# All queries formed ahead of the first iteration, and the last stores on one queue: an attention block with its gradients on one core

## The chip, the core and the metric

The kernel runs on one NeuronCore of a Trainium2 chip. The core has five engines, each with its own instruction queue, that meet only at semaphores: TensorE (PE; its weight loads are shown apart, as PEld), VectorE (DVE), ScalarE (ACT), GpSimd (POOL) and SyncE (SP). Data moves between HBM and the on-chip memory (SBUF) by 16 DMA engines, which serve several queues; here SP's DMAs run in queue q1, ScalarE's in q10 and GpSimd's, whose descriptors are made by software, in q0. TensorE writes to PSUM, eight banks for each partition.

The metric is the time of one execution in microseconds of device time, the median of several runs. Lower is better.

## What is computed

One decode step (one new token for each of two sequences) of a pre-norm transformer block, and its gradients for everything that was put in. Cut to what matters:

```python
B, Sq, D = 2, 1, 640; H, Sk, Dh = 32, 4096, 128; Dff = 1728      # all in bf16
q = layernorm(x) @ wq                       # wq: 640 x 4096, 32 heads of 128
s = q . k_cache * Dh**-0.5                  # for each sequence and head, over 4096 keys
p = softmax(s);  o = p . v_cache
h = x + o @ wo
out = h + relu(layernorm(h) @ w1) @ w2
# and the vector-Jacobian product with grad_out for x, k_cache, v_cache, wq, wo, w1, w2
```

The caches k and v are 2 x 32 x 4096 x 128 each, 1 MB for each pair of sequence and head, and so are their gradients (outputs 2 and 3). These four arrays are nearly all of the bytes moved. Output 0 is the block's result and output 1 the gradient of x, both 2 x 640; outputs 4 to 7 are the gradients of the four weights.

## The kernel before

The program is written out by hand: a planner in Python walks over two interleaved loops and emits each engine's instructions in the order that it fixes. There are 64 pairs (sequence, head).

The first loop (`p1_iter(i)`, 66 iterations) is the forward pass. For pair i it turns the K tile (128 x 4096, 1 MB) over by 32 transposes on TensorE in four groups of eight (`transpose_group`, L418, copied out by ScalarE at L423 or VectorE at L421), multiplies each by the query (`matvec_group`, L429, which reads a column of `qc`) and takes the maximum (L575). One iteration later the scores of that pair become exponentials (L528) and K is scaled by them (`pk_half`, L480). Two iterations later V is multiplied with that (`m_part`, L473). So iteration i needs K of pair i, K of pair i - 1 and V of pair i - 2.

The second loop (`p2_iter(j)`) writes the gradients of the caches. It begins at iteration 41 of the first loop, at every second iteration, and runs alone after the first has ended. For pair j it reads V again (tile W, unless it was kept), turns it over (`pair_transpose`, L439, copied by ScalarE at L444), multiplies it (L452), and forms the tiles gV (of pair j) and gK (of pair j - 1) on VectorE in halves (`outer_half`, L834). GpSimd makes the small tile `pp` (L872) that gV is formed from; VectorE makes `gsp` (L856) for gK. `store_tile` (L839 to 846) sends each tile to HBM.

Between these, other generators run in the gaps: `middle_gen` (the MLP and the second layer norm of a sequence), `ga_gen`, `fin_gen` (outer products for outputs 4 to 7, stored by ScalarE from tiles `ot`), and `gx_gen`, which reads wq a second time in five tiles `wqs` (L989) and multiplies them on VectorE (L660, tile gxj) for output 1. `store_row` (L649 to 655) turns a column over and stores it as a row of output 0 or 1.

The large tiles are places in a pool of twelve, more later, divided by use: "ld" for loads, "g" for gK and gV, "f" and "q" for the others. `take` gets the place given back longest ago, and `give` returns it. A load into a place waits until the tile before it has been read, and VectorE, when it forms gK or gV, until the store of the tile that was there has landed.

All large loads are in one list, `queue`, in the order in which they are wanted, and `pump` issues from its head on SP as long as a place for loads is free: for each iteration K of pair i and V of pair i - 2, with W tiles, w2 in three pieces (iterations 8, 13, 18), wo in four and w1 (iterations 10, 15, 20, 24, 35).

wq is read in six pieces, each with the columns of six heads (`QP = 6`, the last with two): `load_wq` takes one place for loads and moves five chunks of 768 columns for each partition, runs of 1536 B. The first stands at the head of `queue`, and each other one three iterations ahead of its use. `q_piece(k)`, at iterations 0, 6, 12, 18, 24 and 30, forms the queries of its heads in 30 matmuls (L384; 10 for the last), copies them to `qc` and, scaled, to `qsc` (L388, L389), and gives the place back.

Where a store is sent from depends on the list: as long as anything is left in `queue`, gK and gV are stored by GpSimd, and once all loads are issued, by SP. Two of the last gK tiles are then stored in two parts, 120 rows and 8 rows. The rows of outputs 0 and 1 are stored by GpSimd. Engines work through their queues in order, so a store behind which another instruction stands holds that up until the tile is ready.

Of the kernel before, what the change touches and what calls it, by code (L numbers as in the profile page):

```python
# [7 lines left out]
FP32 = mybir.dt.float32  # L8
BF16 = mybir.dt.bfloat16
ALU = mybir.AluOpType  # L10
# [5 lines left out]
def kernel(  # L16
# [20 lines left out]
    nc = tc.nc  # L37

    B, Sq, D = A_x.shape
    _, H, Sk, Dh = A_k_cache.shape  # L40
    HD = A_wq.shape[1]
    Dff = B_w1.shape[1]
    assert (B, Sq, Dh) == (2, 1, 128) and H * Dh == HD
    ND = D // 128
# [4 lines left out]
    SCALE = 0.08837890625  # L49
# [17 lines left out]
    small = ctx.enter_context(tc.tile_pool(name="small", bufs=3))  # L67
# [5 lines left out]
    def pst(shape, dtype, role, name):  # L73

        k = banks[role].pop(0)
        banks[role].append(k)
        return ps.tile(shape, dtype, tag=f"bank{k}", bufs=1, name=name)
# [11 lines left out]
    def take(tag, shape, name):  # L89
        assert free[tag] > 0, (tag, name)  # L90
        free[tag] -= 1
        k = homes[tag].pop(0)
        t = pools[k].tile(shape, BF16, tag=f"big{k}", bufs=1, name=name)
        home_of[id(t)] = (tag, k, t)
        return t
# [9 lines left out]
    def give(t, to=None):  # L105
        tag, k, _ = home_of.pop(id(t))
        to = to or goes_to(tag)
        owned[tag] -= 1
        owned[to] += 1
        free[to] += 1  # L110
        homes[to].append(k)
        given_at[k] = step[0]
# [35 lines left out]
    ident_bf = const.tile([128, 128], BF16)  # L148
# [32 lines left out]
    x1c = cols.tile([128, ND, B], BF16)  # L181
# [11 lines left out]
    qsc = cols.tile([128, H, B], BF16)  # L193
# [133 lines left out]
    qc = pkp.tile([128, H, B], BF16)  # L327
# [36 lines left out]
            nc.sync.dma_start(out=t[0:F_rem, NFF - c0, :], in_=B_w2[NFF * 128:Dff, :])  # L364
        return t

    QP = 6
    NQ = -(-H // QP)
    wq_r = A_wq.rearrange("(c p) n -> p c n", p=128)
    wq_tiles = {}  # L370

    def load_wq(k, tag):
        hn = min(QP, H - k * QP)
        t = take(tag, [128, ND, QP * 128], "wq_t")
        nc.sync.dma_start(out=t[:, :, 0:hn * 128], in_=wq_r[:, :, k * QP * 128:(k * QP + hn) * 128])
        wq_tiles[k] = (t, tag)

    def q_piece(k):
        hn = min(QP, H - k * QP)
        t, tag = wq_tiles.pop(k)  # L380
        q_ps = pst([128, QP, B], FP32, "mid", "q_ps")
        for j in range(hn):
            for c in range(ND):
                nc.tensor.matmul(q_ps[:, j, :], lhsT=t[:, c, j * 128:(j + 1) * 128], rhs=x1c[:, c, :],  # L384
                                 start=(c == 0), stop=(c == ND - 1))
        give(t)
        hs = slice(k * QP, k * QP + hn)
        nc.vector.tensor_copy(out=qc[:, hs, :], in_=q_ps[:, 0:hn, :])  # L388
        nc.vector.tensor_scalar(out=qsc[:, hs, :], in0=qc[:, hs, :], scalar1=SCALE, scalar2=None, op0=ALU.mult)  # L389


    pairs = [(b, h) for b in range(B) for h in range(H)]
    NP1 = len(pairs)
# [61 lines left out]
    def natural(cache, b, h):  # L455
        return cache[b, h].rearrange("(p sc) d -> p sc d", sc=NSC)
# [192 lines left out]
    def store_row(col_bf, n, dst):  # L649

        t = pst([16, 128], BF16, "mid", "row_ps")
        nc.tensor.transpose(t[0:n, :], col_bf, ident_bf[:])
        r = small.tile([16, 128], BF16, tag="orow", bufs=2, name="orow")
        nc.vector.tensor_copy(out=r[0:n, :], in_=t[0:n, :])
        nc.gpsimd.dma_start(out=dst, in_=r[0:n, :])

    def ttr(in0, in1, acc, width, kc=128, junk=None):
        if junk is None:
# [177 lines left out]
            in0=row.rearrange("p (a two) -> p a two", two=2)[:, None, :, :].to_broadcast([128, HALF, 64, 2]),  # L836
            in1=colp[:, sl, None, :].to_broadcast([128, HALF, 64, 2]), op=ALU.mult)

    def store_tile(dst, t, uneven=False):  # L839

        eng = nc.gpsimd if queue else nc.sync
        if uneven:
            eng.dma_start(out=dst[0:120], in_=t[0:120])
            eng.dma_start(out=dst[120:128], in_=t[120:128])
        else:
            eng.dma_start(out=dst, in_=t[:])  # L846

    def p2_iter(j, busy):

        c = S2[j] if j < NP1 else None  # L850
        p = S2[j - 1] if j >= 1 else None
        if p is not None:
            bp, hp = turns[j - 1]
            pair_matvec(p["dp"], p.pop("T3"), 3, gom[:, hp, bp, :, :])
            gsp = small.tile([128, NSC, 2], BF16, tag="gsp", name="gsp")
            nc.vector.scalar_tensor_tensor(  # L856
                out=gsp[:], in0=p["dp"][:, :, None].to_broadcast([128, NSC, 2]), scalar=negdot[:, hp, bp:bp + 1],
                in1=P_bf[:, bp * H + hp, :, None].to_broadcast([128, NSC, 2]), op0=ALU.add, op1=ALU.mult)
        if c is not None:
            b, h = turns[j]  # L860
            go = gom[:, h, b, :, :]

            bank = pst([128, 512], FP32, "sps", "dp_ps")
            for k, col in enumerate((goc, qsc)):
                nc.tensor.matmul(bank[:, 128 + k * 128:256 + k * 128],  # L865
                                 lhsT=col[:, h, b:b + 1].to_broadcast([128, 128]), rhs=ident_bf[:],
                                 start=True, stop=True)
            c["dp"] = bank[:, 0:NSC]
            rb = mats.tile([128, 256], BF16, tag="rb", bufs=4, name="rb")
            nc.scalar.activation(out=rb[:], in_=bank[:, 128:384], func=ACT.Copy, scale=rt[:, b, h:h + 1])  # L870
            pp = small.tile([128, NSC, 2], BF16, tag="pp", name="pp")
            nc.gpsimd.tensor_copy(out=pp[:], in_=P_bf[:, b * H + h, :, None].to_broadcast([128, NSC, 2]))  # L872
            c.update(rb=rb, pp=pp)
            c["T0"] = pair_transpose(c["W"], 0, busy=busy)
        if p is not None:
            gK = take("g", [128, NSC, 128], "gK")
            outer_half(gK, p["rb"][:, 128:256], gsp, 0)
        yield
        if p is not None:
            outer_half(gK, p["rb"][:, 128:256], gsp, 1)  # L880
            store_tile(natural(out_2, bp, hp), gK, NP1 - 3 <= j - 1 < NP1 - 1)
            give(gK)
            del S2[j - 1]
        yield
        if c is None:
            return
        c["T1"] = pair_transpose(c["W"], 1, busy=busy)
        pair_matvec(c["dp"], c.pop("T0"), 0, go)
        yield
        c["T2"] = pair_transpose(c["W"], 2, busy=busy)  # L890
        pair_matvec(c["dp"], c.pop("T1"), 1, go)
        yield
        c["T3"] = pair_transpose(c["W"], 3, busy=busy)
        give(c["W"], "g" if j < H and j != 1 and owned["g"] < 3 else None)
        pair_matvec(c["dp"], c.pop("T2"), 2, go)
        gV = take("g", [128, NSC, 128], "gV")
        outer_half(gV, c["rb"][:, 0:128], c["pp"], 0)
        yield
        outer_half(gV, c["rb"][:, 0:128], c["pp"], 1)
        store_tile(natural(out_3, b, h), gV)  # L900
        give(gV)
        yield

# [178 lines left out]
    i = j = 0  # L1082
    while i <= NP1 + 1 or j <= NP1:
        ii = i if i <= NP1 + 1 else None
# [7 lines left out]
    queue = []  # L1092
    W_AT = (10, 15, 20, 24, 35)
    W2_AT = (8, 13, 18)
    for n, (ii, jj) in enumerate(plan):
        if ii is not None:
            if ii % QP == 3 and (ii + 3) // QP < NQ:
                queue.append(("wq", (ii + 3) // QP))
            if ii < NP1:
                queue.append(("K", ii))  # L1100
        if ii is not None and ii >= 2:
            queue.append(("V", ii - 2))
        ahead = plan[n + 1][1] if n + 1 < len(plan) and ii is not None else jj
        if ahead is not None and ahead < NP1 and turns[ahead] not in kept and ("W", ahead) not in queue:
            queue.append(("W", ahead))
        if ii in W_AT:
            queue.append(("w", W_AT.index(ii)))
        if ii in W2_AT:
            queue.append(("w2", W2_AT.index(ii)))
    queue.insert(0, ("wq", 0))  # L1110
    def pump():
        while queue:
            what, k = queue[0]
            if what == "w":
                load_weights(k)
            else:
                tag = "ld"
                if free["ld"] < 1:
                    return
                if what == "wq":  # L1120
                    load_wq(k, tag)
                elif what == "w2":
                    w2_tiles[k] = load_w2(k, tag)
                else:
                    load_tile(what, k, tag)
            queue.pop(0)

    pump()
    q_piece(0)
    pump()  # L1130
    fin = big1 = big2 = big3 = None
    g2 = None
# [9 lines left out]
            g2 = None  # L1142

    for n, (i, j) in enumerate(plan):
        if i is not None and i % QP == 0 and 1 <= i // QP < NQ:
            q_piece(i // QP)
            pump()
        all_go = all(("go", B - 1, h) in done for h in range(H))
        if i is None and plan[n - 1][0] is not None:
            pkp.release()  # L1150
# [39 lines left out]
        if i is None:  # L1190
            spread[0] = 2
            at_k[0] = 1
            k = 0
# [71 lines left out]
```

## Time and profile before

| | |
|---|---|
| median of 3 runs | 919.53 us (918.83 to 919.62) |
| the profiled execution | 918.83 us |
| its span, first to last instruction | 916.8 us |
| busy: PE, PEld, DVE, ACT, POOL | 747.8, 626.5, 693.5, 531.0, 169.0 us |
| moved by DMA | 363.00 MB, mean 396 GB/s |
| of it q1 (SP), q0 (GpSimd), q10 (ScalarE) | 226.86, 119.55, 14.91 MB |
| loads of wq pieces, 960 KB: issue to landing | median 16.4 us |
| loads of K and V tiles, 1024 KB | 14.8 and 14.7 us |
| stores of gV and gK by GpSimd, 57 each | 13.3 and 13.8 us |
| stores of gV by SP, 7 | 10.7 us |
| mean granted clock of TensorE | 0.782 |

The times of the instructions are from the one profiled execution; the times of day in it are counted from the start of its span, and they are told in microseconds. "PEclk" is the share of its full clock that TensorE was granted. The DMA share is the mean busy share of the 16 DMA engines. A tile "lands" when the semaphore of its DMA is complete, which takes all of the engines that carry a part of it.

### The profile page before, as it was taken

Reading aid. Unit: us, or ns where it says so; the run is one execution under the profiler, and the core shown is the slowest. Engines: PE = TensorE matmul, PEld = TensorE weight load, DVE = VectorE, ACT = ScalarE, POOL = GpSimd, SP = SyncE. Lnnn points to the kernel's source line nnn. Section 1 sums busy time; section 2 is a strip of 40 time slices with the busy share of each in tenths; the row PEclk is TensorE's granted clock in tenths of the full one; section 3 lists DMA queues with packets and bytes.
Section 4 is the critical chain, followed back from the end, with each engine's and each line's share of the span. In section 5 each row is a group of like instructions: output and inputs, shape, how many; then the busy total and the mean of one; then the engine's idle time right before and its main releaser. Section 6 shows DMA issues by size and latency. Waiting matters only on the chain.

```text
span 916.8 us, 26507 instructions
## 1 busy us (share of the span) xinstructions
PE 747.8 (82%) x11226; PEld 626.5 (68%) x11226; DVE 693.5 (76%) x1291; ACT 531.0 (58%) x1096; POOL 169.0 (18%) x319
## 2 busy tenths in 40 slices
PE   5998898999998998998956936885799779868762
PEld 5887787888877787787746835764667566646452
DVE  4655786877879787686879698986898449999774
ACT  3665554567777777676633534544576656637641
POOL 1222222223201111010012111111222111121110
PEclk9999999999999999898987676656555655555555
DMA  9999999999889999999999999999999999999987
GB/s 346 419 394 411 407 395 409 413 418 368 310 287 349 421 422 423 422 422 422 411 410 388 408 425 413 398 408 391 392 404 386 425 424 424 421 425 422 424 338 244
DMA packets 59580, 363.00 MB, mean 396 GB/s; under 512 B 5798, under 2 KB 15654, under 8 KB 19270
## 3 DMA queue, kind: packets, MB, share of 16 engines
q1 hardware_dynamic: 39910, 226.86, 61.9%
q0 software_dynamic: 16544, 119.55, 31.5%
q10 hardware_dynamic: 3008, 14.91, 4.2%
q8 instruction: 88, 1.44, 0.6%
q14 instruction: 30, 0.25, 0.1%
HBM read 212.16 MB, written 149.13 MB: 394 GB/s over the span
## 4 chain that ended last, share of the span: by engine, by line
PE 39%; DMA 26%; DVE 19%; ACT 9%; issue 6%; DVEq 0%; SPq 0%; POOL 0%; ACTq 0%; POOLq 0%
DMA Vt<-in_A_v_cache_dram 12%; PE t_ps L439 8%; PE m_ps L473 8%; PE t_ps L418 7%; DMA out_dram<-gK 7%; DVE gV L834 5%; DMA out_dram<-gV 4%; DVE gK L834 4%; ACT t_sb L423 4%; PE s_ps L429 3%; PE u_ps L502 3%; DMA wqs<-in_A_wq_dram 2%; DVE junk L660 2%; PE o_ps L947 2%; DVE pk L480 2%
## 5 line engine op out<-in xcount | busy, mean ns | idle before, releaser
L423 ACT COPY t_sb<-t_ps 128x1024 bf16<-128x1024 bf16 x223 | 217.7, 1018 | 45.9 <-PE t_ps L418 45.6
L444 ACT COPY t_sb<-t_ps 128x512 f32<-128x512 f32 x256 | 149.8, 588 | 144.7 <-PE t_ps L439 141.8
L480 DVE TENSOR_TENSOR pk<-Kt,ep 128x2048 bf16<-128x2048 bf16 x128 | 156.3, 1221 | 56.8 <-ACT ep L528 27.1
L439 PE MATMUL t_ps<-ident_f,Wt 128*128 128x128 f32 x848 | 197.4, 380 | 1.4 <-ACT t_sb L423 1.4
L473 PE MATMUL m_ps<-pk,Vt 128*128 128x129 bf16 x2048 | 171.4, 222 | 13.3 <-DMA Vt<-in_A_v_cache_dram 11.8
L834 DVE TENSOR_TENSOR gV<-rb,pp 128x2048 bf16<-128x2048 bf16 x128 | 153.1, 1220 | 23.9 <-DMA out_dram<-gK 21.6
L834 DVE TENSOR_TENSOR gK<-rb,gsp 128x2048 bf16<-128x2048 bf16 x128 | 152.4, 1225 | 21.5 <-DMA out_dram<-gV 19.7
L418 PE MATMUL t_ps<-ident_bf,Kt 128*128 128x128 bf16 x2048 | 154.0, 224 | 10.2 <-DMA Kt<-in_A_k_cache_dram 5.2
L439 PEld LDWEIGHTS t_ps<-ident_f,Wt 128*128 128x128 f32 x848 | 136.1, 197 | 35.1 <-issue 28.5
L473 PEld LDWEIGHTS <-Vt 128*128 128x128 bf16 x2048 | 124.8, 99 | 43.8 <-issue 30.2
L418 PEld LDWEIGHTS <-Kt 128*128 128x128 bf16 x2048 | 126.5, 100 | 18.1 <-issue 9.0
L452 PEld LDWEIGHTS <-t_sb 128*128 128x128 bf16 x2048 | 97.0, 107 | 44.3 <-issue 18.9
L452 PE MATMUL dp_ps<-gom,t_sb 128*128 128x2 bf16 x2048 | 95.6, 168 | 9.1 <-ACT t_sb L444 8.0
L490 POOL COPY pk<-ep 128x16 bf16<-128x16 bf16 x80 | 62.8, 786 | 192.2 <-ACT ep L528 158.1
L429 PE MATMUL s_ps<-qc,t_sb 128*128 128x1 bf16 x2048 | 88.2, 164 | 1.4 <-DVE t_sb L421 1.1
L429 PEld LDWEIGHTS <-t_sb 128*128 128x128 bf16 x2048 | 77.7, 97 | 4.1 <-DVE t_sb L421 1.3
L953 ACT CAST ot<-o_ps 128x512 bf16<-128x512 f32 (+4 forms) x160 | 70.3, 489 | 16.9 <-DMA out_dram<-ot 11.0
L846 POOL DMA_DIRECT2D out_dram<-gV x57 | 30.6, 536 | 254.4 <-DVE gV L834 201.3
L846 POOL DMA_DIRECT2D out_dram<-gK x57 | 30.4, 534 | 240.7 <-DVE gK L834 191.0
L870 ACT ACTIVATE rb<-dp_ps,rt 128x256 bf16<-128x256 f32 x64 | 30.4, 476 | 58.9 <-PE dp_ps L865 57.5
L587 ACT CAST MT<-m_ps 128x128 bf16<-128x128 f32 x64 | 17.1, 268 | 73.8 <-PE m_ps L473 73.7
L660 DVE CUSTOM_DVE_ANT_0 junk<-wo_t,hbc 128x640 bf16<-128x640 bf16 x64 | 52.4, 819 | 0.2
(195 smaller groups left out, 786.8 us busy)
## 6 DMA issues: line engine op xcount, KB each, us to landing
Kt<-in_A_k_cache_dram SPq DMA_DIRECT2D x64, 1024.0 KB, 14.8
Vt<-in_A_v_cache_dram SPq DMA_DIRECT2D x64, 1024.0 KB, 14.7
out_dram<-gV POOLq DMA_DIRECT2D x57, 1024.0 KB, 13.3
out_dram<-gK POOLq DMA_DIRECT2D x57, 1024.0 KB, 13.8
Wt<-in_A_v_cache_dram SPq DMA_DIRECT2D x53, 1024.0 KB, 13.8
out_dram<-gV SPq DMA_DIRECT2D x7, 1024.0 KB, 10.7
wo_t<-in_A_wo_dram SPq DMA_DIRECT2D x4, 1280.0 KB, 19.4
wqs<-in_A_wq_dram SPq DMA_DIRECT2D x5, 1024.0 KB, 21.5
```

Source lines behind the costliest of these rows:

```text
L418: nc.tensor.transpose(t_ps[:, j, :], nat[:, g * GT + j, :], ident_bf[:])
L423: nc.scalar.copy(out=t_sb[:], in_=t_ps[:])
L429: nc.tensor.matmul(dst[:, sc:sc + 1], lhsT=t_sb[:, j, :], rhs=vec, start=True, stop=True)
L439: nc.tensor.transpose(t_ps[:, j, :], natf[:, 2 * cc:2 * cc + 2, :].rearrange("p c k -> p (c k)"), ident_f[:])
L444: nc.scalar.copy(out=t_sb[:], in_=t_ps[:])
L452: nc.tensor.matmul(dst[:, sc:sc + 2], lhsT=v[:, j, :, par], rhs=vecs[:, par, :], start=(par == 0), stop=(par == 1))
L473: nc.tensor.matmul(r["m"][:, 0:129], lhsT=r["V"][:, sc, :], rhs=r["pk"][sc // HALF][:, sc % HALF, 0:129], start=(sc == 0), stop=(sc == NSC ...
L480: nc.vector.tensor_tensor(out=p["pk"][k][:, :, 0:128].rearrange("p s (a two) -> p s a two", two=2), in0=p["K"][:, sl, :].rearrange("p s (a ...
L490: nc.gpsimd.tensor_copy(out=col, in_=e)
L660: nc.vector.tensor_tensor_reduce(out=junk[0:kc, 0:width], in0=in0, in1=in1, scale=1.0, scalar=0.0, op0=ALU.mult, op1=ALU.add, accum_out=acc)
L834: nc.vector.tensor_tensor(out=pairs_view(dst[:, sl, :]), in0=row.rearrange("p (a two) -> p a two", two=2)[:, None, :, :].to_broadcast([128 ...
L953: nc.scalar.copy(out=ot[0:P, k, n0:n0 + nn], in_=o_ps[0:P, 0:nn])
```

## The change

Three things change.

The queries: the six pieces go. `all_q` first issues five loads, each a chunk of 128 rows of wq with all 4096 columns, so that each partition reads one run of 8 KB, into five places for loads. They stand ahead of everything in `queue`, and 32 matmuls for each tile then add up the queries of all heads in one PSUM bank, ahead of the first iteration. As the 32 heads' sums in the bank are open at the same time, a matmul with a tile of zeros begins them and only the last one of all ends them. One copy and one scaling of all heads follow.

The stores: `store_tile` goes. All gK and gV tiles are stored by GpSimd, each in one part.

The rows of outputs 0 and 1 are stored by SP in place of GpSimd.

```diff
-    QP = 6
-    NQ = -(-H // QP)
     wq_r = A_wq.rearrange("(c p) n -> p c n", p=128)
-    wq_tiles = {}
-
-    def load_wq(k, tag):
-        hn = min(QP, H - k * QP)
-        t = take(tag, [128, ND, QP * 128], "wq_t")
-        nc.sync.dma_start(out=t[:, :, 0:hn * 128], in_=wq_r[:, :, k * QP * 128:(k * QP + hn) * 128])
-        wq_tiles[k] = (t, tag)
-
-    def q_piece(k):
...
+    def all_q():
+
+        zero = small.tile([128, H * B], BF16, tag="zero", bufs=1, name="zero")
+        nc.vector.memset(zero[:], 0.0)
+        tiles = []
+        for c in range(ND):
+            t = take("ld", [128, HD], "wq_t")
+            nc.sync.dma_start(out=t[:], in_=wq_r[:, c, :])
+            tiles.append(t)
+        yield
+        q_ps = pst([128, H, B], FP32, "mid", "q_ps")
+        nc.tensor.matmul(q_ps[:].rearrange("p h b -> p (h b)"), lhsT=ident_bf[:], rhs=zero[:], start=True, stop=False)
+        for c, t in enumerate(tiles):
+            for h in range(H):
+                nc.tensor.matmul(q_ps[:, h, :], lhsT=t[:, h * 128:(h + 1) * 128], rhs=x1c[:, c, :],
+                                 start=False, stop=(c == ND - 1 and h == H - 1))
+            give(t)
+        nc.vector.tensor_copy(out=qc[:], in_=q_ps[:])
+        nc.vector.tensor_scalar(out=qsc[:], in0=qc[:], scalar1=SCALE, scalar2=None, op0=ALU.mult)
+        yield
...
-        nc.gpsimd.dma_start(out=dst, in_=r[0:n, :])
+        nc.sync.dma_start(out=dst, in_=r[0:n, :])
...
-    def store_tile(dst, t, uneven=False):
-
-        eng = nc.gpsimd if queue else nc.sync
-        if uneven:
-            eng.dma_start(out=dst[0:120], in_=t[0:120])
-            eng.dma_start(out=dst[120:128], in_=t[120:128])
-        else:
-            eng.dma_start(out=dst, in_=t[:])
-
...
-            store_tile(natural(out_2, bp, hp), gK, NP1 - 3 <= j - 1 < NP1 - 1)
+            nc.gpsimd.dma_start(out=natural(out_2, bp, hp), in_=gK[:])
...
-        store_tile(natural(out_3, b, h), gV)
+        nc.gpsimd.dma_start(out=natural(out_3, b, h), in_=gV[:])
...
-            if ii % QP == 3 and (ii + 3) // QP < NQ:
-                queue.append(("wq", (ii + 3) // QP))
...
-    queue.insert(0, ("wq", 0))
...
+    first_q = all_q()
+    next(first_q)
     pump()
-    q_piece(0)
+    next(first_q)
     pump()
...
-        if i is not None and i % QP == 0 and 1 <= i // QP < NQ:
-            q_piece(i // QP)
-            pump()
```

More of the change, by code (lines that the diff above doesn't have):

```diff
@@ L365, in load_w2 @@
         return t
-    QP = 6
-    NQ = -(-H // QP)
     wq_r = A_wq.rearrange("(c p) n -> p c n", p=128)
-    wq_tiles = {}
-    def load_wq(k, tag):
-        hn = min(QP, H - k * QP)
-        t = take(tag, [128, ND, QP * 128], "wq_t")
-        nc.sync.dma_start(out=t[:, :, 0:hn * 128], in_=wq_r[:, :, k * QP * 128:(k * QP + hn) * 128])
-        wq_tiles[k] = (t, tag)
-    def q_piece(k):
[L379 to L389, printed above, removed]
+    def all_q():
[17 more added lines that the diff above has]
+        yield
     pairs = [(b, h) for b in range(B) for h in range(H)]
@@ L1119, in pump @@
                     return
-                if what == "wq":
-                    load_wq(k, tag)
-                elif what == "w2":
+                if what == "w2":
                     w2_tiles[k] = load_w2(k, tag)
```

## The prediction

> **What bounds the kernel now.** I read the page's row of slices first, then the stretches, then the time line of TensorE's waits and the chain of waits for the end.
>
> ```profile
> DMA  9999999999889999999999999999999999999987
> GB/s 346 419 394 411 407 395 409 413 418 368 310 287 349 421 422 423 422 422 422 411 410 388 408 425 413 398 408 391 392 404 386 425 424 424 421 425 422 424 338 244
> ```
>
> The reader is to see that the DMA engines are the bound in two long stretches (slices 1 to 9 and 14 to 38), and that two places fall out: slices 10 to 13 and the last two. The same by stretches (columns: window, length, busy us of PE, PEld, DVE, ACT, POOL, granted clock, DMA share, GB/s):
>
> ```profile
> 206.00:298.00 92.00, 85.08 (x1687) 75.08 (x1685) 72.92 (x189) 67.67 (x131) 19.55 (x33) 1.00 0.87 329
> 298.00:850.00 552.00, 441.92 (x5649) 363.96 (x5650) 446.24 (x760) 324.60 (x697) 86.39 (x170) 0.70 1.01 413
> 850.00:870.00 20.00, 14.79 (x115) 9.35 (x113) 14.26 (x23) 11.46 (x23) 2.88 (x3) 0.59 1.01 423
> 870.00:890.00 20.00, 12.68 (x107) 9.09 (x107) 12.24 (x21) 9.02 (x18) 0.98 (x2) 0.50 0.80 329
> 890.00:893.00 3.00, 3.00 (x25) 2.43 (x24) 2.97 (x5) 1.50 (x3) 1.24 (x2) 0.50 0.98 399
> 893.00:908.00 15.00, 6.37 (x79) 5.66 (x77) 10.41 (x11) 4.00 (x7) 3.13 (x2) 0.61 0.98 315
> ```
>
> From 206 to 298 us the DMAs have slack and compute sets the pace, so a shift of the first stage passes through it whole. From 298 to 850 the bytes set the pace (413 GB/s), the same bytes before and after, so the shift passes again. After 850 the end depends on how the stores drain. So two places have to be priced: the first 206 us and the last 65.
>
> The first stage, TensorE's time line (start, length, instruction, wait before it):
>
> ```profile
> 8.87 0.94 PE L384 MATMUL q_ps<-x1c,wq_t 128*128 128x2 bf16 x30 [3.44 <-DVE x1c L273]
> 9.67 1.87 PE L418 MATMUL t_ps<-ident_bf,Kt 128*128 128x128 bf16 x16
> ...
> 72.15 1.07 PE L418 MATMUL t_ps<-ident_bf,Kt 128*128 128x128 bf16 x16 [0.74 <-DMA Kt<-in_A_k_cache_dram]
> 75.99 0.73 PE L473 MATMUL m_ps<-pk,Vt 128*128 128x129 bf16 x8 [2.71 <-DMA Vt<-in_A_v_cache_dram]
> 107.42 1.07 PE L418 MATMUL t_ps<-ident_bf,Kt 128*128 128x128 bf16 x16 [1.12 <-DMA Kt<-in_A_k_cache_dram]
> 109.92 0.64 PE L473 MATMUL m_ps<-pk,Vt 128*128 128x129 bf16 x8 [1.38 <-DMA Vt<-in_A_v_cache_dram]
> 141.09 1.77 PE L418 MATMUL t_ps<-ident_bf,Kt 128*128 128x128 bf16 x16 [2.54 <-DMA Kt<-in_A_k_cache_dram]
> 143.53 1.05 PE L473 MATMUL m_ps<-pk,Vt 128*128 128x129 bf16 x8 [0.57 <-DMA Vt<-in_A_v_cache_dram]
> 159.81 0.89 PE L384 MATMUL q_ps<-x1c,wq_t 128*128 128x2 bf16 x30
> 160.56 1.05 PE L418 MATMUL t_ps<-ident_bf,Kt 128*128 128x128 bf16 x16
> ```
>
> TensorE is almost always busy, but stops three times for a late K and V tile, in iterations 11, 16 and 21. By the starts of the maximum at L575 (71.61 to 81.80, 106.33 to 115.10, 138.59 to 148.62) these took 10.2, 8.8 and 10.0 us instead of the usual 5.7: stops of 4.5, 3.1 and 4.3. The last two lines show what a piece of queries costs on this chain: 160.56 - 159.81 = 0.75 us.
>
> The end, from the DMA queues between 869 and 884 us (packets, MB, share) and from the chain of waits:
>
> ```profile
> q1 hardware_dynamic: 476, 3.42, 55.1%
> q10 hardware_dynamic: 481, 1.81, 29.8%
> q0 software_dynamic: 39, 0.26, 4.4%
> ```
> ```profile
> 848.67 34.77 DMA out_dram<-gK
> ```
>
> A store of 1 MB is 128 packets of 8 KB. The last POOL store (queue q0) is issued at 848.67 and lands 34.8 us later, yet in the last 15 us q0 moves 39 packets in all: most engines are long done with it, and one or two that lag hold it open, serving SP's newer stores (q1, landing after 10.7 to 11.3 us) in turn with the old ones. VectorE waits for exactly these old tiles, which is why the DMA share falls to 0.80.
>
> **Part 1, wq first.** Six pieces (5.24 MB, runs of 1536 B) become five tiles of 1.05 MB in rows of 8 KB, on SP's queue ahead of the first K tile. At 420 GB/s (the second slice) a tile takes 2.5 us. Before, the first piece has arrived at 7.0 us (TensorE's first weight load of it) and K0 some 2.5 later, in time for 9.67. After, the five tiles end at 7.1 + 4 x 2.5 = 17.1 and K0 at 19.6: the first iteration starts 9.9 us later. The 160 matmuls (4.75 us busy, so 0.95 per tile of 32) hide in the 2.5 us between tiles, the last 0.95 under K0's transfer; so do the added zero matmul, the memset (0.07) and the two wide copies (0.17 each). If that cover were gone they cost 1.3 us once. Removed from TensorE's chain: four pieces of 0.75 at iterations 6, 12, 18, 24 and a third of one at 30, 3.25 in all.
>
> Now the offset, iteration by iteration. Where the kernel before stops for a tile, the new offset is the larger of (offset minus the stop) and the lateness of the tile, which is 12.5 us for all wq less 2.5 for each piece already moved by then. Start +9.9; after iteration 6 +9.15. Iteration 11: max(9.15 - 4.5, 12.5 - 7.5) = +5.0; at 12, +4.25. Iteration 16: max(4.25 - 3.1, 12.5 - 10.0) = +2.5; at 18, +1.75. Iteration 21: max(1.75 - 4.3, 0) = 0. At 24, -0.75; at 30, **-1.0**. The long packets could save up to 0.2 us a piece (slice 3, 394 GB/s, against 420), 1.2 in all; I count none. Ends: -3.6 (iteration 21 bound by the chain) and +6.6 (no stop shortened: 9.9 - 3.25). The load slots are no limit: SP issues a tile 15 us (median) before it lands.
>
> **Part 2, the last stores.** Fourteen stores stay on POOL's queue, and two gK stores lose their split into 120 and 8 rows. Issue: 14 x 0.53 on POOL for 0.33 on SP, behind a backlog, nothing. POOL works in order, so the pp copy (L872, 0.41, but 1.63 and 2.71 beside a busy VectorE at 889 and 893) now stands behind the gV store: 0.53 + 2.71 against the 2.64 that VectorE spends on gsp and gK, up to 0.6 late in each of 6 iterations. Hidden by the six or seven stores in flight; without them 3.6 us.
>
> The drain: everything issued before 885 has landed at 889.9 (the last ot store, issued at 878.50, took 11.4). After it the kernel before still has eight stores and ends its last one at 915.3 (SP's issue to 905.7, then its wait of 9.6 for that store). All in one queue, oldest first, VectorE no longer waits for a tile that newer stores overtook, so the lagging engine always has work, and it has the same work. Eight stores at 399 GB/s (plain stores, 890 to 893) take 21.0: 910.9, where now the split ones run at 315. That is **-4.4**. Ends: if no engine lagged, the 13.7 MB left at 870 would go at 423 GB/s and end at 902.5 (-12.8); if the split did relieve the lagging engine, it gets 16 packets more, two stores' share of 2.5 each (+5.0). I take the value between, as the lag is in the rows and the slow packets are too.
>
> The Trainium skill ("DMA: Bandwidth & Descriptors", SWDGE vs HWDGE vs iDMA) speaks against this part: GpSimd writes its descriptors into SBUF, where VectorE's fast modes can lock it out, and SP's path is immune. The trace shows POOL's issues at 0.53 to 0.54 us from 840 to 850 with VectorE 99% busy, so nothing of it there. If each of 14 issues waited for one VectorE instruction (1.22), that would be 17 us on top of the sum below: 931.
>
> **Part 3, the rows.** Output rows go to SP. The two of out_0 (ready at 814.1 and 814.7) now stand ahead of the fifth wqs load, issued at 809.69 before: 5.3 us later. Its first reader on VectorE is at 828.18; at 15.4 us to landing (the Wt issued just before it) it comes at about 830, a wait of up to 4 us. The Wt loads behind that one are issued from 821.48 in any case. The backlog of POOL stores (28 us from issue to landing there) hides it: 0, at worst +4. The rows of out_1 have nothing behind them.
>
> **Sum.** 916.8 - 1.0 - 4.4 = 911.4 span; the profiled execution is 2.0 longer than its span (918.83), and the median 0.7 above that one: **914.1**.
>
> **Rivals.** (a) The lagging engine decides: with the split gone it has two more shares, and 893 to 908 is slow because it is stores only. Speaks for it: the share is 0.98 there; against: 399 GB/s just before, stores too. It decides if the last stores' landing is set by q0's oldest packets: +5.0 - 1.0, 923.5. (b) The late start isn't paid back: tiles arrive later than I count, or the slots run dry, and the stops stay. +6.6 - 4.4, 921.7; against it: DMA share 1.02 and the queue's 15 us. (c) The queue makes no difference, as the bytes are the same: -1.0 alone, 918.5.
>
> **Chances.** Forecast 0.50, (a) 0.20, (b) 0.13, (c) 0.17. The forecast alone spans 909 to 918 (the packets' 1.2 and half the way to the tail's better end below; the 4 us of part 3 above). The range reaches down to 908 and up to (a), 923.5. A difference of 0.2% (1.8 us) is about what can be told from none. Faster 0.52 (the forecast less 0.03, and 0.05 of (c)), same 0.18, slower 0.30.
>
> **What would show it.** L418's first matmul near 19.6 us; waits for K and V gone at iteration 11, and one left near 141; the middle reached 1 us earlier (iteration 34's maximum, 224.59 before); no L384-like piece between iterations. In the tail q0 near 400 GB/s, DMA share near 1.0 from 850 to 905, last landing near 910. I am wrong if iteration 34 comes later than before, or if the last POOL stores land more than 15 us after their issue with most engines idle.

## The result, and the profile after

The changed kernel takes 909.85 us (median of 4 runs, 908.67 to 913.75) against 919.58 for the kernel before (918.83 to 921.13): a ratio of 0.9899, 95% interval 0.9866 to 0.9933. The forecast was 914.1. Run again later on another chip, nine times beside 28 runs of the kernel before (below), the same kernel stood at 0.9941 [0.9919, 0.9962]. So it is faster, by 6 to 10 us, which is 0.6 to 1.0%. The profiled execution took 910.81 us, with a span of 908.6.

The start first. TensorE's time line of the kernel after (start, length, instruction, the wait before it):

```profile
8.91 1.87 PE L383 MATMUL q_ps<-x1c,wq_t 128*128 128x2 bf16 x64
11.37 1.01 PE L383 MATMUL q_ps<-x1c,wq_t 128*128 128x2 bf16 x32 [0.59 <-DMA wq_t<-in_A_wq_dram]
...
17.66 1.01 PE L383 MATMUL q_ps<-x1c,wq_t 128*128 128x2 bf16 x32 [2.79 <-DMA wq_t<-in_A_wq_dram]
20.17 1.14 PE L416 MATMUL t_ps<-ident_bf,Kt 128*128 128x128 bf16 x9 [1.50 <-DMA Kt<-in_A_k_cache_dram]
...
142.29 0.64 PE L471 MATMUL m_ps<-pk,Vt 128*128 128x129 bf16 x8 [1.36 <-DMA Vt<-in_A_v_cache_dram]
...
166.01 0.64 PE L471 MATMUL m_ps<-pk,Vt 128*128 128x129 bf16 x8 [1.01 <-DMA Vt<-in_A_v_cache_dram]
```

The queries are formed in the gaps between the five tiles, and the first K tile is turned over at 20.17 us in place of 9.67. The stops for late K and V tiles in iterations 11 and 16 are gone; two are left, at 142 and 166. By the starts of the maximum (L573, L575 before) the offset against the kernel before goes: +10.1 us at iteration 0 and again at 10 (9.7 to 10.9 between), +5.4 at 11, +2.1 at 16, +1.3 at 20, -1.8 at 21, -1.9 at 34 (222.67 against 224.59).

Now the end: stretches of the span (us, length, busy time and instructions of PE, PEld, DVE, ACT and POOL, then granted clock, DMA share and GB/s).

```profile
850.00:870.00 20.00, 15.14 (x105) 9.57 (x105) 19.01 (x32) 11.01 (x22) 3.31 (x7) 0.50 1.02 426
870.00:890.00 20.00, 16.02 (x174) 12.83 (x172) 16.25 (x22) 10.80 (x20) 4.03 (x10) 0.67 1.01 422
890.00:893.00 3.00, 0.00 (x0) 0.00 (x0) 2.20 (x2) 0.00 (x0) 0.94 (x2) 0.54 1.01 423
893.00:908.00 15.00, 0.00 (x0) 0.00 (x0) 0.00 (x0) 0.00 (x0) 0.03 (x1) 0.50 0.46 192
```

From 870 to 890 the DMAs are full (1.01 and 422 GB/s, where it was 0.80 and 329). The last gK store is issued at 892.50, 11 us earlier, and lands at 906.8 in place of 915.3. In the last 15 us every engine is idle and under half of the DMA engines are at work: the shares of the last store land one after another from 897.5 to 906.8. At the 423 GB/s of the row above, the 2.9 MB that are left at 893 (192 GB/s over 15 us) would have been gone by about 900; by this estimate the uneven end still costs some 7 us.

The waits of VectorE for stores between 850 and 900 us (in us, times, longest):

```profile
DVE gK L832 <- DMA out_dram<-gV: 1.2, 1, 1.2
DVE gV L832 <- DMA out_dram<-gK: 0.7, 1, 0.7
```

In the kernel before, the same view from 850 to 906 has these lines:

```profile
DVE gV L834 <- DMA out_dram<-gK: 8.7, 3, 3.8
DVE gK L834 <- DMA out_dram<-gV: 4.5, 3, 2.6
```

13.2 us of waiting for stores have become 1.9. That looks like the whole explanation, but the experiments show that most of these waits can come back while the time stays. One line of the chain of waits after is a hint: a gK store can still be open for 31 us, though all stores are in one queue now.

```profile
823.57 30.96 DMA out_dram<-gK
854.65 1.23 DVE gV L832
```

### The profile page after: what moved, and what is told of

The parts are those of the page before. It is cut to its first block, busy times and chain, and to the rows that moved or that the text cites. A ratio compares the mean times of both kernels' runs of the same rounds, so it can differ in the third digit from the quotient of the medians.

```text
span 908.6 us, 26495 instructions
## 1 busy us (share of the span) xinstructions
PE 740.8 (82%) x11227; PEld 620.3 (68%) x11227; DVE 692.1 (76%) x1282; ACT 530.7 (58%) x1096; POOL 173.1 (19%) x329
## 4 chain that ended last, share of the span: by engine, by line
PE 36%; DMA 27%; DVE 18%; ACT 9%; issue 7%; POOL 0%; SPq 0%; POOLq 0%; ACTq 0%; DVEq 0%
DMA out_dram<-gK 11%; DMA Vt<-in_A_v_cache_dram 10%; PE m_ps L471 9%; PE t_ps L416 8%; PE t_ps L437 6%; DVE gV L832 5%; ACT t_sb L421 4%; DVE gK L832 4%; PE s_ps L427 4%; DVE junk L658 3%; PE u_ps L500 3%; DMA wqs<-in_A_wq_dram 3%; DMA out_dram<-gV 2%; DVE pk L478 2%; DMA Kt<-in_A_k_cache_dram 2%
## 5 line engine op out<-in xcount | busy, mean ns | idle before, releaser
L437 PE MATMUL t_ps<-ident_f,Wt 128*128 128x128 f32 x848 | 190.9, 371 | 1.0 <-ACT t_sb L421 1.0
L437 PEld LDWEIGHTS t_ps<-ident_f,Wt 128*128 128x128 f32 x848 | 131.4, 191 | 32.4 <-issue 26.1
L488 POOL COPY pk<-ep 128x16 bf16<-128x16 bf16 x80 | 64.9, 812 | 188.2 <-ACT ep L526 159.9
L889 POOL DMA_DIRECT2D out_dram<-gV x64 | 34.3, 536 | 277.0 <-DVE gV L832 198.3
L870 POOL DMA_DIRECT2D out_dram<-gK x64 | 34.1, 533 | 253.6 <-DVE gK L832 196.5
```

The source lines that it names most:

```text
L437: nc.tensor.transpose(t_ps[:, j, :], natf[:, 2 * cc:2 * cc + 2, :].rearrange("p c k -> p (c k)"), ident_f[:])
L488: nc.gpsimd.tensor_copy(out=col, in_=e)
```

## The experiments

Twelve runs, in three groups of four. Each group ran on one chip, beside the kernel before (medians 918.54, 918.47 and 918.65), so ratios are compared, and times within a group.

**1. The parts alone.** The queries at once, with the stores and rows of the kernel before (edits are shown against the changed kernel here, and against the kernel before in the next one):

```diff
-            nc.gpsimd.dma_start(out=natural(out_2, bp, hp), in_=gK[:])
+            store_tile(natural(out_2, bp, hp), gK, NP1 - 3 <= j - 1 < NP1 - 1)
...
-        nc.sync.dma_start(out=dst, in_=r[0:n, :])
+        nc.gpsimd.dma_start(out=dst, in_=r[0:n, :])
```

> Part 1 alone (wq first, all queries at once), stores and rows as before. Theory: the late start is paid back by the stops at iterations 11, 16 and 21 and by the pieces removed. The maximum of iteration 34 comes 1.9 us earlier than before (224.6), as in the changed kernel, the tail is as before (SP's stores beside old ones in q0, slow split ones), and the time is 919.6 - 1.9 = 917.7, ratio 0.998; up to 916 if the 1.8 us that the changed kernel gained between 298 and 850 us belongs to this part. Rival: the gain is all in the first part, and the stores are only issued elsewhere: 910 to 911, ratio 0.990.

Measured: 916.15 us, ratio 0.9978 [0.9959, 0.9998]; iteration 34 at 222.6. The stores and rows alone, with the queries in six pieces as before:

```diff
-            store_tile(natural(out_2, bp, hp), gK, NP1 - 3 <= j - 1 < NP1 - 1)
+            nc.gpsimd.dma_start(out=natural(out_2, bp, hp), in_=gK[:])
...
-        nc.gpsimd.dma_start(out=dst, in_=r[0:n, :])
+        nc.sync.dma_start(out=dst, in_=r[0:n, :])
```

> Parts 2 and 3 alone (all gK and gV stores by GpSimd in one part, rows by SP), queries in pieces as before. Theory: the first 850 us are as before (iteration 34 at 224.6, three stops), and in the tail the DMA share stays near 1.0 to the last store, which lands some 5 us earlier: 919.6 - 4.9 = 914.7, ratio 0.995. Rival (the bytes are the same whoever issues the store): 919.6, ratio 1.000. Second rival (the relief of the split is lost): slower, 923 or more.

Measured: 915.34 us, 0.9971 [0.9949, 0.9992]; iteration 34 at 223.9, the DMAs full to 900 us. Both parts gain a little, and neither is the whole.

**2. The split.** The kernel before, its last stores still on SP, without the parting into 120 and 8 rows:

```diff
-            store_tile(natural(out_2, bp, hp), gK, NP1 - 3 <= j - 1 < NP1 - 1)
+            store_tile(natural(out_2, bp, hp), gK)
```

> The kernel before with one edit: SP's last gK stores go in one part of 128 rows, not 120 and 8. Theory: the slow packets after 893 us come from the split (120 rows over the engines in another pattern); without it the last 15 us run near 400 GB/s in place of 315 and the time falls by about 3 us, to 916.5. The waits of VectorE for old tiles of q0 between 865 and 885 stay. Rival: the slow packets come from stores alone, and the split relieved the engine that lags: the packets stay slow and the time rises by 3 to 5 us, to 923 to 925.

And the reverse, the changed kernel with the two split stores put back, on GpSimd:

```diff
+            if NP1 - 3 <= j - 1 < NP1 - 1:
+                nc.gpsimd.dma_start(out=natural(out_2, bp, hp)[0:120], in_=gK[0:120])
+                nc.gpsimd.dma_start(out=natural(out_2, bp, hp)[120:128], in_=gK[120:128])
```

> The changed kernel with the split put back, on GpSimd's queue: two gK stores in 120 and 8 rows. Theory (the split disturbs the packets whoever issues it): the last 15 us fall from about 400 to 315 GB/s and the time rises by 3 us, to about 913. Rival (the split takes work from the engines that land last, 4 us after the others): the last landing comes 2 to 5 us earlier, 905 to 908.

Measured: without the split 915.05 us, 0.9956 [0.9929, 0.9983]; with it put back 916.99, 0.9980 [0.9960, 1.0001]. The stretch from 884 to 900 us of the kernel before without the split:

```profile
884.00:900.00 16.00, 9.73 (x103) 8.27 (x100) 13.84 (x16) 5.63 (x10) 4.83 (x3) 0.61 1.02 425
```

and of the changed kernel with it:

```profile
884.00:900.00 16.00, 4.96 (x58) 4.31 (x58) 7.71 (x9) 3.17 (x6) 2.91 (x6) 0.61 0.99 333
```

The DMA share is about 1 in both, but 425 GB/s against 333: the engines are as busy and carry less, so single packets take longer. Of the traces' packets of 8 KB in this stretch, nine of ten take at most 309 to 333 ns in the kernels without a split by rows; with one the median is still 309 to 316, but the slowest tenth takes some 600 ns and more. The change itself, whose DMAs run empty before 900 us, has 396 GB/s in this stretch at a share of 0.95. The split costs time wherever it is issued. The unsplit stores on SP gain as much as those on GpSimd, within the intervals.

**3. Queue, rows, and a load moved.** The change itself once more, for comparison:

> The changed kernel itself, to have it on one chip beside the next three. Theory (the split alone had slowed the end, and the shorter query stage gives 2 us): 0.989 to 0.993 of the kernel before, iteration 34's maximum 1.9 us earlier than before, the last data landing 6 to 9 us earlier. If the two parts only add up as they did one by one (0.9978 and 0.9971 or 0.9956), it is 0.993 to 0.995.

Measured: 912.44 us, 0.9941 [0.9919, 0.9962]; iteration 34 at 222.9. The two parts add up within the intervals (0.9978 x 0.9971 = 0.9949, or 0.9934 with the 0.9956 of the split alone). Next, the last stores back on SP and the rows on GpSimd, without a split:

```diff
+        eng = nc.gpsimd if queue else nc.sync
+        eng.dma_start(out=dst, in_=t[:])
```

> The queries at once and no split, but the last stores on SyncE's queue and the output rows on GpSimd's, as before. Theory (the split was the whole of the stores' gain): within 0.3% of the changed kernel, DMA share about 1.0 from 870 to 900. Rival (my prediction's own reason: in one queue, oldest first, the lagging engines are fed evenly): 3 to 5 us slower than the changed kernel, with a DMA share under 0.9 in 870 to 890.

Measured: 911.67 us, 0.9928 [0.9904, 0.9953], no difference from the change. From the run with the queries alone (0.9978) this kernel differs in the split and nothing else. Here VectorE's waits from 850 to 900 are back:

```profile
DVE gK L832 <- DMA out_dram<-gV: 5.1, 2, 2.9
DVE gV L832 <- DMA out_dram<-gK: 4.2, 2, 3.4
```

9.3 us of waits, and the last store is issued 8.6 us later than in the change's first profile and 7.3 later than in its second (901.13 against 892.50 and 893.83, by the traces). Yet it lands at 908.5, against 906.8 and 908.1. The windows of this kernel:

```profile
870.00:890.00 20.00, 14.33 (x121) 10.84 (x121) 13.50 (x23) 9.48 (x19) 2.13 (x2) 0.50 0.91 372
884.00:900.00 16.00, 12.45 (x133) 10.77 (x133) 15.90 (x20) 6.81 (x12) 5.35 (x4) 0.61 0.98 400
```

The reader is to see that two things offset each other. From 870 to 890 the DMAs carry 0.9 MB less than in the change beside it (372 against 417 GB/s, a share of 0.91 against 1.01), as the rival said, and at 893 they have 5.0 MB left, where the change has 3.0 (333 against 200 GB/s over the last 15 us). But the last store on SP needs 7.4 us to land, and its sixteen shares land within 3.4 us of each other; the change's last store needs 14.2 to 14.3, and its shares are 9.3 us apart. So the waits come back, stores are issued later, and the last one lands no later. On balance the queue is worth nothing here; what the waits would cost without the evener end isn't shown.

The four output rows on GpSimd again:

```diff
-        nc.sync.dma_start(out=dst, in_=r[0:n, :])
+        nc.gpsimd.dma_start(out=dst, in_=r[0:n, :])
```

> The changed kernel with the four output rows issued by GpSimd again, so that they stand among its stores. Theory (my part 3: the rows' queue is worth nothing): within 0.2% of the changed kernel. Rival (a row that waits for its values holds GpSimd's stores up): the stores of the last ten iterations 1 to 4 us later, 0.2 to 0.4% slower.

Measured: 912.94 us, 0.9949 [0.9929, 0.9969], which is 0.05% from the change. The stores of the last six iterations leave 0.5 to 0.6 us later than in the change beside it (894.3 against 893.8 for the last one); those from 805 to 849 us left 4.3 later, but that began before the first row (815.08).

Two quarters of wo, four iterations later:

```diff
-    W_AT = (10, 15, 20, 24, 35)
+    W_AT = (10, 15, 24, 28, 35)
```

> The changed kernel with the third and fourth quarter of wo loaded at iterations 24 and 28, not 20 and 24: 2.6 MB out of the way of the V tiles for which TensorE still stops at 142.29 (1.36 us) and 166.01 (1.01 us). Theory (bytes ahead of 206 us set this stage, and its offset passes to the end): both stops gone, iteration 34's maximum 1.5 to 2.4 us earlier than in the changed kernel, the end 1 to 2.4 us earlier. Rival (the offset at 34 is lost by the end, as DMA bytes are the same): the maximum earlier, the end within 0.5 us.

Measured: 911.79 us, 0.9930 [0.9908, 0.9953]. Iteration 21 is 1.6 us earlier than in the change beside it (145.8 against 147.4), as the tiles ahead of it no longer queue behind the third quarter. But the stop of iteration 25 is only put off, to where the quarters now stand:

```profile
187.15 0.64 PE L471 MATMUL m_ps<-pk,Vt 128*128 128x129 bf16 x8 [1.20 <-DMA Vt<-in_A_v_cache_dram]
```

Iteration 34 starts at 221.5, 1.4 us earlier, but the span ends only 0.6 earlier and the time falls by 0.65 us, which the runs don't resolve.

**4. Which split, and what the first part is made of.** The same two gK stores in two halves of the rows, then in two halves of every row:

```diff
+                nc.gpsimd.dma_start(out=natural(out_2, bp, hp)[0:64], in_=gK[0:64])
+                nc.gpsimd.dma_start(out=natural(out_2, bp, hp)[64:128], in_=gK[64:128])
```

> The changed kernel with the same two gK stores split into rows 0 to 63 and 64 to 127. Theory (rows that are dealt to the DMA engines in another order than in a whole store are slow, as with 120 and 8): from 890 to 900 about 310 to 350 GB/s, last data 3 to 5 us later than in the changed kernel. Rival (only the pieces of half a row, 4 KB, that 120 rows over 16 engines leave are at fault, which 64 rows do not have): 390 to 425 GB/s there and within 0.2% of the changed kernel.

```diff
+                nc.gpsimd.dma_start(out=natural(out_2, bp, hp)[:, 0:HALF, :], in_=gK[:, 0:HALF, :])
+                nc.gpsimd.dma_start(out=natural(out_2, bp, hp)[:, HALF:NSC, :], in_=gK[:, HALF:NSC, :])
```

> The changed kernel with the same two gK stores split into two halves of every row: 128 packets of 4 KB each, every row where it is in a whole store. Theory (the order of the rows is at fault): no slow packets, 390 to 425 GB/s from 885 to 895, within 0.2% of the changed kernel. Rival (two transfers in place of one, or packets under 8 KB, are at fault): about 310 to 350 GB/s, 3 to 5 us later.

Measured: halves of the rows 916.85 us, 0.9974 [0.9949, 1.0]; halves of every row 912.55, 0.9942 [0.9916, 0.9969]. From 884 to 900 us with halves of the rows:

```profile
884.00:900.00 16.00, 4.51 (x50) 3.75 (x48) 7.53 (x8) 2.81 (x5) 2.59 (x6) 0.61 1.01 324
```

and with halves of every row:

```profile
884.00:900.00 16.00, 5.57 (x67) 4.92 (x65) 8.28 (x9) 3.40 (x6) 2.90 (x6) 0.50 1.01 414
```

Two transfers in place of one cost nothing that shows (0.9942 beside the change's 0.9941), nor do packets of 4 KB (159 ns each). What costs is that a store has only a part of the rows: 324 GB/s with 64 rows, 333 with 120 and 8. The 4 KB pieces that the rival supposed aren't there at all: in the split kernel, too, GpSimd's queue has only packets of 8 KB and the few bytes that end a store.

The Trainium skill ("DMA: Bandwidth & Descriptors", The descriptor swizzle) says that in a 1 MiB transfer to 128 partitions each engine writes one port of SBUF. The stores here read from SBUF instead; if they follow the same order, and a part of the rows breaks it, engines would share ports and wait for each other. This would agree with 425 GB/s for whole stores, 414 for halves of every row and 324 for halves of the rows, but the trace doesn't name the engine of a packet, so neither the order nor the sharing is shown.

The early start given back, with the same bytes and, for 26 of the heads, runs of 6.5 KB:

```diff
-    first_q = all_q()
+    first_q = first_heads()
...
+            if 1 <= ii <= ND:
+                queue.append(("wq", ii))
...
+        if i == Q0:
+            other_heads()
```

> The changed kernel with the early start given back: six heads of wq (0.98 MB) first, the first iteration at 15.5 us, the other 26 heads' rows in five tiles among the loads of iterations 1 to 5 and their queries formed at once ahead of iteration 6 (130 matmuls, 3.9 us). Same bytes and same long rows. Theory (what has arrived decides from iteration 21 on, and the start counts for nothing): iteration 5 about 10 us earlier than in the changed kernel, iteration 21 and 34 within 0.7 us of it, the time within 0.3%. Rival (the late start of 10 us still costs): iteration 34 2 to 8 us earlier, 0.3 to 0.8% faster.

Measured: 913.66 us, 0.9944 [0.9921, 0.9966]. The first iteration's maximum is at 14.8 in place of 25.3, at iteration 5 the lead is 5.9 us, and at iteration 10 it is gone (82.0 against 81.7). TensorE's time line of this kernel shows where a part of it goes:

```profile
36.60 0.64 PE L487 MATMUL m_ps<-pk,Vt 128*128 128x129 bf16 x8 [1.37 <-DMA Vt<-in_A_v_cache_dram]
43.60 0.64 PE L487 MATMUL m_ps<-pk,Vt 128*128 128x129 bf16 x8 [1.36 <-DMA Vt<-in_A_v_cache_dram]
...
47.84 3.44 PE L399 MATMUL q_ps<-x1c,wq_t 128*128 128x2 bf16 x130
...
140.82 1.07 PE L432 MATMUL t_ps<-ident_bf,Kt 128*128 128x128 bf16 x16 [0.58 <-DMA Kt<-in_A_k_cache_dram]
143.31 1.05 PE L487 MATMUL m_ps<-pk,Vt 128*128 128x129 bf16 x8 [1.37 <-DMA Vt<-in_A_v_cache_dram]
```

Two stops for V tiles that haven't arrived take 1.4 us each. But iteration 6 alone takes 11.6 us in place of 5.5: the 130 matmuls now stand on TensorE's chain (3.44 us), and the granted clock is 0.50 from 50.4 to 57.2. So the early start bought nothing, as the forecast had it, but this run doesn't show that late tiles alone took it back. The eight profiles of kernels with the change's first stage show the tiles' part better: the starts of the maximum of iteration 20 lie 1.5 us apart (139.6 to 141.0), those of iteration 21, behind the stop near 142, 0.5 us (146.9 to 147.4), and the two latest at 20 (140.9 and 141.0) are among the four earliest at 21 (146.9 and 147.1).

Iteration 34 is at 225.2, 2.5 later than in the change, and this was expected by neither theory. Its windows name the place:

```profile
136.00:140.00 4.00, 4.00 (x95) 3.47 (x93) 3.23 (x6) 1.58 (x4) 1.65 (x3) 1.00 1.02 417
140.00:143.00 3.00, 1.36 (x27) 1.10 (x23) 2.19 (x8) 1.85 (x4) 0.00 (x0) 0.93 1.01 415
143.00:146.00 3.00, 2.69 (x38) 2.69 (x39) 1.24 (x3) 1.41 (x4) 1.31 (x1) 0.50 1.03 423
146.00:150.00 4.00, 4.00 (x53) 2.97 (x51) 2.10 (x4) 0.32 (x1) 1.42 (x2) 0.58 1.02 420
```

After the stops the granted clock is 0.50 and 0.58 for seven us; 3.00 x 0.50 + 4.00 x 0.42 = 3.2 us of TensorE's time, about what was lost between iterations 20 and 21 (+0.4 to +3.3). The kernel before has such a dip in the same place in its profile, 0.71 and 0.72 from 140 to 143 and from 143 to 146, and the two other kernels with the old queries have none (1.00). Iteration 21 took 10.0 us there, against 7.3 and 7.6, but most of that is an earlier arrival at iteration 20 (138.6 against 140.5 and 140.7); at iteration 21 the kernel with the dip is 0.6 us behind the two others.

Last, all six old pieces ahead of the first K tile, in their short runs:

```diff
-            t = take("ld", [128, HD], "wq_t")
-            nc.sync.dma_start(out=t[:], in_=wq_r[:, c, :])
+            t = take("ld", [128, ND, QP * 128], "wq_t")
+            nc.sync.dma_start(out=t[:, :, 0:hn * 128], in_=wq_r[:, :, k * QP * 128:(k * QP + hn) * 128])
```

> The changed kernel with wq in the six old pieces of heads (runs of 1536 B), but all six ahead of the first K tile and the queries formed at once. Theory (the gain at iteration 34 is the pieces that TensorE no longer forms after iteration 21): start and iteration 34 within 0.5 us of the changed kernel, time within 0.2%. Rival (it is the shorter transfer of whole rows): start and iteration 34 1 to 2 us later, as in the kernel before at 34, 0.1 to 0.25% slower.

Measured: 915.38 us, 0.9950 [0.9923, 0.9976]. K0 is turned over at 22.13 in place of 20.17, and iteration 34 starts at 224.7 in place of 222.7: the 2.0 us go through unchanged. They are the short runs: at 22.13 TensorE has waited 2.06 us for K0 itself, with the queries done. The first stretch of this kernel:

```profile
2.00:20.00 18.00, 6.46 (x165) 5.91 (x165) 4.12 (x26) 0.03 (x1) 1.54 (x9) 1.00 1.02 345
```

and of the changed kernel:

```profile
2.00:20.00 18.00, 6.27 (x166) 5.72 (x166) 4.56 (x29) 0.03 (x1) 1.55 (x9) 1.00 0.99 397
```

345 against 397 GB/s over 18 us is 0.94 MB, 2.2 us at the later rate. The rival of this run was right as to the place, in one profile; the time can't be told from the change's within these intervals.

No version ran faster than the change beyond its interval: the ones with SP's stores and with the later wo (911.67 and 911.79) are equal to it (912.44).

## Why the prediction was right, point by point

**What bounds the kernel** held for the first stage. The rule for the offset (the larger of the old offset less the stop, and the lateness of the tile) gave +9.9, +5.0 at 11, +2.5 at 16 and 0 at 21; the traces show +10.1, +5.4, +2.1 and -1.8. The stops were read a little wrong, from one usual length of 5.7 us (without long stops these iterations take 5.5, 6.3 and about 6.0), but in each of the three it was the lateness of the tile that set the rule's value. Of the last, about 0.6 us goes with the dip of the clock in the first profile: against the two other kernels with the old queries (148.0 and 148.1 at iteration 21; 146.9 and 147.4 in the change's two profiles) it is -0.9. The kernel before starts 10 us earlier and loses that lead at its stops for tiles; from iteration 21 on arrival decides, not the start. Rival (b), a late start that isn't paid back, falls. That the shift then passes to the end whole is not shown (below).

**Part 1, -1.0**: the sum had it from the pieces that TensorE no longer forms at iterations 24 and 30, and counted none of the up to 1.2 us from longer packets. That step failed in its reason. The pieces did go: iteration 24 takes 6.1 us in place of 6.9, iteration 30 takes 5.8 in place of 6.0, together the 1.0. But TensorE, 1.0 us earlier, now runs into a V tile at 166.01 and waits 1.01 us for it: iteration 25 takes 6.4 in place of 5.4, and from iteration 21 to 34 it is 75.8 us as it was (75.8 to 76.0; 75.5 to 76.1 in the eight profiles with the new queries). What was gained is the long rows: all pieces ahead in short runs put iteration 34 at 224.7, long rows at 222.6 to 223.2 in eight profiles, some 2 us where the sum has 0. The three profiles with the old queries have 224.6, 223.9 and 223.9, so part 1 gives about -1.3 at this place. In the time it is 0.9978, or 2.0 us, and 0.9941 against 0.9956 between the unsplit kernels, 1.4 us. That the term came out near its size, with a reason that gained nothing, is luck.

**Part 2, -4.4**: the size was near (the change at 0.9941 against 0.9978 without its stores is 3.4 us; taking only the split away gave 4.0), one of its two reasons failed. The prediction said that in one queue, oldest first, VectorE no longer waits for a tile that newer stores overtook, so that the lagging engine always has work. VectorE's waits did go, 13.2 us to 1.9, but with the last stores on SP and 9.3 us of those waits the time is the same: what the DMAs lose from 870 to 890 is made up by an end that is more even. And in one queue some engines still lag: the shares of the last store land over 9.3 us. What was paid for is the other half of the sentence, eight stores at the rate of plain ones: 425 against 333 GB/s. It had that slow rate on the page (315 GB/s from 893) and took it as a share of the term; it is the term, as far as the runs can tell. Both terms together were -5.4, and 914.1 is 0.9941 of the kernel before, just what the later group measured; with one reason gone in each part, that closeness is partly luck.

**Rival (a)**, that the split had relieved the lagging engine, falls: putting it back costs 0.9980 / 0.9941, some 3.6 us. **Rival (c)**, that the queue makes no difference, was right about the queue, on balance, and wrong about the time, since it forgot the split. **Part 3, 0**: the rows' queue makes a difference of 0.05%, which the runs don't resolve. The 17 us that the prediction estimated from what the Trainium skill ("DMA: Bandwidth & Descriptors", SWDGE vs HWDGE vs iDMA) says of VectorE locking out GpSimd's descriptor writes did not appear: with VectorE 19.01 of 20 us busy from 850 to 870, GpSimd's store issues keep their mean of 0.53 to 0.54 us, and GpSimd and SP as the last queue give the same time. The trace doesn't tell in which mode VectorE ran.

**What would show it**: the first K matmul near 19.6 was at 20.17; the stop left near 141 was at 142, and one more at 166, on which the pieces' gain was lost, was not foreseen. In the tail q0 was to run near 400 GB/s: all queues together moved 422 to 423 from 870 to 893. The share near 1.0 to 905 was wrong: from 893 on it is 0.46, as some engines end 9 us before others. The last landing, forecast near 910, came at 906.8 and 908.1, 14.3 and 14.2 us after its issue with most engines idle, just short of the 15 us that the prediction named as a sign of being wrong.

**What stays open**: the first group of runs shows 9.7 us, the later one 6.0; the intervals overlap and nothing in the two profiles (spans 908.6 and 909.8) separates them. Between iterations 34 and 800 us the offset wanders by 2 to 4 us from run to run, so whether the gain at 34 reaches the end whole is not resolved by any single profile.

## What to carry to other kernels

When a wait disappears together with time, put the wait back alone before you believe it was the cause: here 9 us of it came back and the time stayed, as the last transfers ended more evenly. Where a stretch is bound by transfers, read GB/s beside the share of busy time: full share at 320 GB/s beside full share at 425 means slow packets, and it named the cost (two stores parted by rows) that the waits did not. And in a stage that waits for tiles, what mattered here is the rate at which bytes arrive, thus long runs, more than when the first iteration starts or how many matmuls are left out.

## What the runs showed of the hardware that was not expected

- A 1 MB store of 128 rows of 8 KB, parted by rows (120 and 8, or 64 and 64), slows the traffic around it to 324 to 333 GB/s with the DMA engines 99 to 101% busy; parted in halves of every row, it runs at 414.
- With wq in runs of 1536 B the loads came at 345 GB/s from 2 to 20 us, with wq in runs of 8 KB at 397, with the same share of busy time (1.02 and 0.99).
- After two stops of 0.58 and 1.37 us TensorE's granted clock was 0.50 and 0.58 for 7 us, a further loss of about 3 us; in another kernel the same two stops (0.59 and 1.35) were followed by a clock of 1.00. What sets the dip off wasn't tried.
- The sixteen shares of the change's last store land over 9.3 us, and of one store up to 15.9 us apart (21.4 in the kernel before). A store can stay open for 31 us with all stores in one queue, and for 35 with two.
